# The second chunk of the first pass: from plain products to Strassen's seven, with its order around the first chunk's second stage and the sixth transposition

## The chip, the cores and the metric

One core of a Trainium2 chip. TensorE (PE in the profile, with its weight loads as PEld) does the matrix products, VectorE (DVE), ScalarE (ACT) and GpSimd (POOL) the elementwise work, and SyncE (SP) issues nearly all DMAs. The metric is device microseconds of one execution; the times of the kernel before are given as a median of four runs. Everything is fp32.

## The reference, cut to what matters

Causal attention with a decay and no softmax (8 batches, 8 heads, 576 tokens, 64 wide), whose output, 4608 tokens by 512, goes through a feed-forward block with a hidden width of 2048.

```python
scores = scale * np.matmul(q, k.transpose(0, 1, 3, 2))
Dmat = np.where(rel >= 0, gamma[:, None, None] ** rel[None, :, :], 0.0)
ret = np.matmul(scores * Dmat[None, :, :, :], v)
x = ret.transpose(0, 2, 1, 3).reshape(B * S, H * D)
h = x @ w_in
sp = np.maximum(h, 0.0) + np.log1p(np.exp(-np.abs(h)))
g = h * erf(sp)
return g @ w_out
```

## The kernel before, in words

**Attention.** The 4608 tokens are cut into 36 pieces of 128, numbered from 0. Each piece goes through three stages in a fixed list (`stages`): `transposes(i)` brings q and k into transposed form (qT, kT), `scores(i)` multiplies them on PE (L347, eight matmuls) and masks the product on DVE into sT (L352, recorded at L99), and `outputs(i)` makes the piece's output on PE (L365, L376, L388) and writes it, scaled, into the tile x on DVE. `attend` runs the list up to a given place. For pieces 0 to 7, q and k are transposed on PE (L332) and copied out by ACT; from piece 8 on, q is transposed on DVE in squares of 32 (L326), and from piece 12 on k too. `weigh_values(i)` multiplies v by a decay on POOL (L313): for pieces 0 to 7 inside `transposes(i)`, later inside `outputs(i - 1)`. Each call also issues the loads of a later piece on SP's queue. The sixth transposition is that of piece 5.

**Feed-forward.** Four pieces make a chunk of 512 tokens; there are nine chunks. The hidden width is done in four groups (g) of 512 columns, so there are 36 blocks (g, c); "the first pass" is g = 0, which runs while attention still makes x. Each block has a first stage (x times w_in, L496) and a second stage (times w_out, L604), between them ACT's Softplus and Erf (L565, L569) and DVE's product of the two (`multiply`).

**Strassen.** Both stages run as a 2 by 2 block product in seven block products (the Winograd form) in place of eight. One product is four 128x256 matmuls. It needs sums of blocks of x (`operands_x`: four DVE instructions for g = 0, each 128x512, the third of them in place) and sums of blocks of the weights (`sums_in`, `sums_out`: four each per group). `First.first`, `middle` and `last` issue the products in the order A11, A12; S2, S3, S1; S4, A22. Three results are added on DVE to what ACT copied out before (L514, L527, L535, recorded at L99). The other way, `First.plain` (L539), makes the eight products as 16 steps of two matmuls (L550) and needs no sums of x or of w_in. Before the change chunks 0 and 1 of the first pass are plain (`PLAIN = 2`), so what is stored of them for the later passes (`xd`) is x without sums, and a later pass makes all three sums of the four that are not stored.

**Weights.** w_in and w_out come as float64 words and are rounded to fp32 in a generator, `rounding`, one step at a time: two ACT instructions (L254, L255), then DVE steps at L259, L263, L267 and L272, then two products, on DVE for the first group's w_in and on POOL for the rest (L274, L275). Behind the last part of a weight stand its block sums as four more steps. `round_weights(n)` takes n steps. In the first group the sums of w_out (wb) come ahead of those of w_in (wa), both behind the last part of w_out.

**Order.** All engines run in the order in which the program issues: there is no scheduler. The order around the change is written by hand: the string at L754 (a: one attention stage; p: one plain step of chunk 0; digits: rounding steps; w: a load of weights; s: store of x; k: filling matmuls), and the loop at L774 to L784, which runs chunk 1's 16 plain steps with one attention stage at every second one and issues chunk 0's Softplus, Erf, `multiply` and `sums` in between. Then chunk 0's second stage starts (`seconds[0].first`), and the general loop at L789 takes over; it catches attention up by `attend(after_chunk(2))` ahead of chunk 2's sums, so that whatever the order was, all stages up to the outputs of piece 11 are out when chunk 2's first product begins.

Of the kernel before, what the change touches and what calls it, by code (L numbers as in the profile page):

```python
# [2 lines left out]

# [1 line left out]

# [49 lines left out]
def kernel(  # L55
# [16 lines left out]
    n_dc = D_MODEL // P  # L72
    OH = D_MODEL // 2
    FH = D_FF // 2
    GP = 2
# [22 lines left out]
    def tt(out, in0, in1, op):  # L98
        nc.vector.tensor_tensor(out=out, in0=in0, in1=in1, op=op)  # L99
# [50 lines left out]
    def load(i, names="qkv"):  # L150
        if i < len(pieces):
            t = loaded.setdefault(i, {})
            for name in names:
                src = {"q": q, "k": k, "v": v}[name]
                if name == "q" and i < SQUARES:
                    t["q"] = load_rows(i, "q", q, 2)
                elif name == "q":
                    t["qs"] = load_squares(i, "q", q)
                    if i >= SQUARES_K:
                        t["ks"] = load_squares(i, "k", k)  # L160
                elif name == "v" or i < SQUARES_K or len(pieces[i]) == 1:
                    t[name] = load_rows(i, name, src, 4)
# [29 lines left out]
    def parts():  # L192

        w2 = w_in.rearrange("(e c d) (h f) -> c e d h f", c=n_dc, d=D, h=2)
        for g in range(n_g):
            for dc in range(n_dc):
                a = A11 if dc < 2 else A12
                src = [(heads[(e + dc) % 2], w2[dc, e, :, :, 2 * g * GW : 2 * (g + 1) * GW]) for e in range(2)]

                yield src, "wa", g, a, dc % 2, ["wa"] if g > 0 and dc == n_dc - 1 else []  # L200
            for f in range(2):
                for j in range(GP):
                    ft = f * FH // P + g * GP + j
                    src = [(slice(0, P), w_out[ft * P : (ft + 1) * P, :].rearrange("p (h o) -> p h o", h=2))]
                    sums = (["wb"] if g > 0 else ["wb", "wa"]) if (f, j) == (1, GP - 1) else []
                    yield src, "wb", g, B21 if f else B11, j, sums

    def sums_in(a11, s3, a12, a22, s1, s2, s4):
# [9 lines left out]
    def sums_out(b11, t3, b21, b22, t1, t2, t4):  # L218
# [7 lines left out]
        yield  # L226

    coming = parts()
    words = []
    most_g = [1]  # L230

    def load_weights():
        part = next(coming, None)
        if part is not None:
            t = wraw.tile([P, 2 * WP], UINT32, tag="wraw", name="wraw")
            for rows, src in part[0]:
                nc.sync.dma_start(out=t[rows].rearrange("p (h f) -> p h f", h=2), in_=src)
            words.append((t, *part[1:]))
# [49 lines left out]
    def round_weights(n=1):  # L288
        for _ in range(n):
            next(round_step, None)  # L290
# [149 lines left out]
    done = [0]  # L440

    def before_chunk(c):

        return stages.index((outputs, c * PC)) if c < n_ch else len(stages)

    def after_chunk(c):

        return stages.index((outputs, (c + 1) * PC - 1)) + 1

    def attend(upto):  # L450
        while done[0] < min(upto, len(stages)):
            of, i = stages[done[0]]
            of(i)
            done[0] += 1

    PLAIN = 2

    def load_x(g, c):  # L460
        x[g, c] = x_tile()
# [2 lines left out]
    def store_x(c):  # L464
        nc.sync.dma_start(out=xd[c], in_=x[0, c][:, :n_dc])
# [3 lines left out]
    def operands_x(g, c):  # L469
        summed.add((g, c))  # L470
        t = x[g, c]
        b11, b12, b21, b22 = (t[:, 2 * d : 2 * d + 2, h * TH : (h + 1) * TH] for d in range(2) for h in range(2))
        t1, t2, t4 = (t[:, n_dc + j, :].rearrange("p (d i) -> p d i", d=2) for j in range(3))
        if g == 0 or c < PLAIN:
            tt(t1, b12, b11, ALU.subtract)
            tt(t2, b22, t1, ALU.subtract)
            tt(b12, b22, b12, ALU.subtract)
        else:
            tt(t2, b12, b11, ALU.add)
            tt(t1, b22, t2, ALU.subtract)  # L480
        if g == 0:
            store_x(c)
        tt(t4, b21, t2, ALU.subtract)
        x[g, c] = {A11: b11, A12: b21, S4: b22, A22: t4, S1: t1, S2: t2, S3: b12}
# [240 lines left out]
    firsts = [First(g, c) for g, c in order]  # L725
    seconds = [Second(f) for f in firsts]
# [8 lines left out]
    def keep_busy(n):  # L735
        for _ in range(n):
            nc.tensor.matmul(idle[:, :P], lhsT=ones, rhs=ones, start=True, stop=True)


    most = [before_chunk(2)]  # L740

    def run(steps, rounds=(), stages=1):

        for step, _ in enumerate(steps):
            attend(min(done[0] + stages, most[0]))
            round_weights(rounds[step] if step < len(rounds) else 0)
# [4 lines left out]

    for what in "alkakakawkakakawwaa3awa2aaa5ppappa5wwppa5ppawappwcppa5ppaaapp5s":  # L754
        if what == "a":
            attend(done[0] + 1)
        elif what == "p":
            next(products)
        elif what == "s":
            store_x(0)  # L760
        elif what == "l":
            load(2, "kv")
        elif what == "c":
            nc.sync.dma_start(out=cst[:, CONST_FIRST:], in_=consts[:, CONST_FIRST:])
        elif what == "w":
            load_weights()
        elif what == "k":
            keep_busy(2)
        else:
            round_weights(int(what))  # L770
    most[0] = before_chunk(3)
    attend(after_chunk(1))
    store_x(1)
    for step, _ in enumerate(firsts[1].plain()):  # L774
        if step % 2 == 0:
            attend(min(done[0] + 1, most[0]))
        round_weights(int(step > 1))
        if step == 1:
            firsts[0].softplus()
            firsts[0].erf()  # L780
        elif step == 5:
            firsts[0].multiply()
        elif step == 8:
            firsts[0].sums()  # L784
    seconds[0].begin()
    run(seconds[0].first(), (2, 2))
    firsts[1].softplus()
    most[0] = before_chunk(4)
    for b, nxt in zip(blocks[2:], blocks[3:] + [None]):  # L789
        n = order.index((b.g, b.c))  # L790
# [9 lines left out]
        elif n + 2 < n_s:  # L800
            f = firsts[n + 1]
# [62 lines left out]
```

## Time and profile before

| what | value |
|---|---|
| median of four runs | 1029.7 us (1028.82 to 1031.45) |
| the profiled execution, its own time | 1031.62 us |
| its span | 1029.8 us |
| PE matmul busy | 1019.5 us, 6348 records |
| PE weight load busy | 876.9 us |
| DVE busy | 668.3 us |
| ACT busy | 390.3 us |
| POOL busy | 123.6 us |
| granted TensorE clock, mean | 0.998 |

How to read it: each fp32 matmul of the program stands in the profile as two MATMUL records. 1.8 us of the profiled execution's time lie outside its span. A matmul record's duration overlaps the next one's, so for the cost of PE work the spacing from start to start is taken. The profile's line numbers are those of the kernel before.

### The profile page before, as it was taken

The numbers are of one execution on the slowest core, as the hardware profiler recorded it, in microseconds if no ns is written. First come the engines' busy times: TensorE is split into PE (matmuls) and PEld (weight loads), VectorE is DVE, ScalarE is ACT, GpSimd is POOL, SyncE is SP. The second block draws the span as 40 slices with busy tenths as digits, with TensorE's granted clock in tenths as the row PEclk, the third lists the DMA queues.
The fourth block names the chain that finished last, engine by engine and source line by source line (L and its number), as shares of the span: only waits on it lengthen the run. The fifth ranks groups of instructions, "written<-read, shape, count | busy, mean of one in ns | idle before, by whom it ended". The sixth has DMA issues, their size and how long they took to land.

```text
span 1029.8 us, 15959 instructions
## 1 busy us (share of the span) xinstructions
PE 1019.5 (99%) x6348; PEld 876.9 (85%) x6348; DVE 668.3 (65%) x1062; ACT 390.3 (38%) x481; POOL 123.6 (12%) x122
## 2 busy tenths in 40 slices
PE   9899999999999999999999999999999999999998
PEld 7687888888888888888888888888888888888887
DVE  3759878877876666666566666666657655555555
ACT  2254133232244544334343344444443333333332
POOL 2133121221311110000001001100100000000000
PEclk9999999999999999999999999999999999999999
DMA  9986979979984444444445344444433334444434
GB/s 197 203 235 147 247 155 246 230 172 244 233 191 151 165 144 143 144 155 166 159 147 170 143 143 144 156 168 147 143 123 123 123 124 131 131 132 131 128 85 120
DMA packets 146986, 165.76 MB, mean 161 GB/s; under 512 B 97376, under 2 KB 121568, under 8 KB 138848
## 3 DMA queue, kind: packets, MB, share of 16 engines
q1 hardware_dynamic: 144832, 163.57, 56.2%
q10 hardware_dynamic: 2080, 1.18, 0.5%
q8 instruction: 50, 0.82, 0.4%
q14 instruction: 24, 0.20, 0.1%
HBM read 117.52 MB, written 47.19 MB: 160 GB/s over the span
## 4 chain that ended last, share of the span: by engine, by line
PE 88%; DMA 4%; DVE 4%; SPq 2%; issue 1%; POOL 1%; ACT 0%; DVEq 0%; POOLq 0%; ACTq 0%
PE a L604 23%; PE a L496 22%; PE g L496 11%; PE g L604 11%; PE e L604 6%; PE e L496 5%; PE s L347 2%; PE o L365 2%; DMA wraw<-in_moe_w_in_dram 1%; PE o L388 1%; PE o L376 1%; SPq L147 1%; DMA raw_qs<-in_q_dram 1%; DMA raw_ks<-in_k_dram 1%; PE f L668 1%
## 5 line engine op out<-in xcount | busy, mean ns | idle before, releaser
L496 PE MATMUL a<-x,wa 128*128 128x256 f32 x1088 | 258.3, 380 | 0.0
L496 PEld LDWEIGHTS a<-x,wa 128*128 128x128 f32 x1088 | 205.7, 190 | 28.5
L604 PE MATMUL a<-wb,s 128*128 128x256 f32 x840 | 200.0, 381 | 0.0
L604 PEld LDWEIGHTS a<-wb,s 128*128 128x128 f32 x840 | 158.4, 190 | 23.0 <-ACT o L618 0.7
L99 DVE TENSOR_TENSOR t<-g,t 128x512 f32<-128x512 f32 x68 | 46.9, 690 | 150.4 <-ACT t L526 112.9
L496 PE MATMUL g<-x,wa 128*128 128x256 f32 x544 | 129.2, 380 | 0.0
L496 PEld LDWEIGHTS g<-x,wa 128*128 128x128 f32 x544 | 102.8, 190 | 14.4
L99 DVE TENSOR_TENSOR o<-a,o 128x512 f32<-128x512 f32 x104 | 71.5, 687 | 46.4 <-PE a L604 46.4
L521 ACT COPY t<-a 128x512 f32<-128x512 f32 x34 | 19.9, 586 | 188.3 <-PE a L496 188.3
L99 DVE TENSOR_TENSOR t<-t,s 128x1024 f32<-128x1024 f32 x72 | 88.9, 1275 | 0.0
L565 ACT ACTIVATE s<-t 128x1024 f32<-128x1024 f32 x72 | 72.1, 1049 | 28.5 <-DVE t L99 28.4
L274 POOL TENSOR_TENSOR wraw<-wraw 128x512 f32<-128x512 f32 x28 | 29.4, 1051 | 439.5 <-DVE wraw L272 177.9
L99 DVE TENSOR_TENSOR x<-x 128x512 f32<-128x512 f32 x115 | 75.8, 693 | 1.2
L532 ACT COPY t<-a 128x512 f32<-128x512 f32 x34 | 19.9, 586 | 144.3 <-PE a L496 144.3
L569 ACT ACTIVATE s<-s 128x1024 f32<-128x1024 f32 x72 | 72.1, 1048 | 0.4
L604 PE MATMUL g<-wb,s 128*128 128x256 f32 x280 | 66.7, 381 | 0.1
L604 PE MATMUL e<-wb,t 128*128 128x256 f32 x280 | 66.6, 380 | 0.0
L604 PE MATMUL a<-wb,t 128*128 128x256 f32 x280 | 66.6, 380 | 0.0
L604 PE MATMUL g<-wb,t 128*128 128x256 f32 x280 | 66.3, 380 | 0.0
L496 PE MATMUL e<-x,wa 128*128 128x256 f32 x272 | 64.8, 381 | 0.0
L99 DVE TENSOR_TENSOR sT<-s,cst 128x512 f32<-128x512 f32 x72 | 46.2, 682 | 28.5 <-PE s L347 28.5
L99 DVE TENSOR_TENSOR o<-g,o 128x512 f32<-128x512 f32 x70 | 47.9, 684 | 21.5 <-ACT o L618 18.8
(86 smaller groups left out, 1251.2 us busy)
## 6 DMA issues: line engine op xcount, KB each, us to landing
od<-o SPq DMA_DIRECT2D x54, 512.0 KB, 3.3
x<-xd SPq DMA_DIRECT2D x27, 1024.0 KB, 4.8
o<-od SPq DMA_DIRECT2D x27, 1024.0 KB, 5.4
raw_qs<-in_q_dram SPq DMA_DIRECT2D x96, 112.0 KB, 4.4
raw_ks<-in_k_dram SPq DMA_DIRECT2D x84, 112.0 KB, 4.1
xd<-x SPq DMA_DIRECT2D x9, 1024.0 KB, 5.2
raw_v<-in_v_dram SPq DMA_DIRECT2D x64, 128.0 KB, 4.5
wraw<-in_moe_w_in_dram SPq DMA_DIRECT2D x32, 256.0 KB, 6.0
```

Of the source, the lines that this page charges most:

```text
L99: nc.vector.tensor_tensor(out=out, in0=in0, in1=in1, op=op)
L147: queue.dma_start(out=t[r0 : r0 + n, e::2, :], in_=heads.rearrange("h p d -> p h d"))
L274: engine.tensor_tensor(out=r_f, in0=high_f, in1=r_f, op=ALU.mult)
L347: nc.tensor.matmul(ps[e][:, p, :], lhsT=t["kT"][heads[e], p, :], rhs=t["qT"][heads[e], p, :], start=True, stop=True)
L365: nc.tensor.matmul(o[p % 2][heads[(e + p) % 2], p // 2, :], lhsT=t["v"][:, 2 * p + e, :], rhs=t["sT"][:, e, p, :], start=(p < 2), stop=(no ...
L376: nc.tensor.matmul(o[p % 2][heads[(e + p) % 2], p // 2, r0 : r0 + m], lhsT=state[heads[e], p, :], rhs=t["qT"][heads[e], p, r0 : r0 + m], s ...
L496: nc.tensor.matmul(acc[:, j * TH : (j + 1) * TH], lhsT=weights["wa", self.g][:, a, d, j * P : (j + 1) * P], rhs=x[self.g, self.c][a][:, d, :],
L521: nc.scalar.copy(out=self.t1[:, 1], in_=self.a)
L532: nc.scalar.copy(out=self.t2[:, 0], in_=self.a)
L565: nc.scalar.activation(self.s[:, j], t, AF.Softplus)
L569: nc.scalar.activation(self.s[:, j], self.s[:, j], AF.Erf)
L604: nc.tensor.matmul(acc[:, tp, :], lhsT=left[:, j * TH + tp * P : j * TH + (tp + 1) * P], rhs=weights["wb", self.g][:, b, j, :], start=(sta ...
```

## The change

Chunk 1's first stage in the first pass goes by the seven products: its 16 plain steps become 7, with one attention stage ahead of each. `operands_x(0, 1)` is issued in front of them; it also stores the chunk, now with the in-place sum in it, so later passes make two sums of this chunk and not three. w_in's sums of the first group stand behind w_in's own last part, and the digit 4 in the string takes them. Chunk 0's Softplus and Erf, `multiply` and `sums` are issued at steps 0, 2 and 4. Softplus of chunk 1 is called by `last` and so comes ahead of chunk 0's second stage. In the string, the two plain steps that stood behind piece 5's transposition (`ppappa`) stand ahead of it (`ppppaa`).

```diff
-                yield src, "wa", g, a, dc % 2, ["wa"] if g > 0 and dc == n_dc - 1 else []
+                yield src, "wa", g, a, dc % 2, ["wa"] if dc == n_dc - 1 else []
...
-                    sums = (["wb"] if g > 0 else ["wb", "wa"]) if (f, j) == (1, GP - 1) else []
+                    sums = ["wb"] if (f, j) == (1, GP - 1) else []
...
-    PLAIN = 2
+    PLAIN = 1
...
-    for what in "alkakakawkakakawwaa3awa2aaa5ppappa5wwppa5ppawappwcppa5ppaaapp5s":
+    for what in "alkakakawkakakawwaa3awa2aaa5ppppaa5wwppa5ppawappwcpp4a5ppaaapp5s":
...
-    store_x(1)
-    for step, _ in enumerate(firsts[1].plain()):
-        if step % 2 == 0:
-            attend(min(done[0] + 1, most[0]))
-        round_weights(int(step > 1))
-        if step == 1:
+    operands_x(0, 1)
+    f = firsts[1]
+    for step, _ in enumerate(chain(f.first(), f.middle(), f.last())):
+        attend(min(done[0] + 1, most[0]))
+        round_weights((0, 2, 2, 2, 2, 3, 3)[step])
+        if step == 0:
             firsts[0].softplus()
             firsts[0].erf()
-        elif step == 5:
+        elif step == 2:
             firsts[0].multiply()
-        elif step == 8:
+        elif step == 4:
             firsts[0].sums()
     seconds[0].begin()
-    run(seconds[0].first(), (2, 2))
-    firsts[1].softplus()
+    run(seconds[0].first())
```

## The prediction

> **What bounds the kernel now.** I read the page's engine table and slices first.
>
> ```profile
> PE 1019.5 (99%) x6348; PEld 876.9 (85%) x6348; DVE 668.3 (65%) x1062; ACT 390.3 (38%) x481; POOL 123.6 (12%) x122
> PE   9899999999999999999999999999999999999998
> ```
>
> PE is the bound, and after the first slices it has no gap to give back: what this change is worth is PE work taken out, plus gaps closed, less gaps opened, between 29 and 104 us. The chain of waits gives the unit: eight records, four matmuls of 128x256, take 1.73 us, or 1.92 us behind an attention stage, so a matmul costs 0.432 us.
>
> Then PE's timeline around the sixth transposition, and, second, the windows of 3.41 us there, whose columns are length, busy time of the five engines with their instruction counts, granted clock, DMA share and GB/s.
>
> ```profile
> 29.70 1.99 PE L550 MATMUL p<-x,wa 128*128 128x256 f32 x8
> 34.34 0.63 PE L332 MATMUL pt_q<-ident,raw_q 128*128 128x128 f32 x4 [2.65 <-DMA raw_q<-in_q_dram]
> 35.56 0.88 PE L332 MATMUL pt_k<-ident,raw_k 128*128 128x128 f32 x4 [0.59 <-DVE wa L275]
> 36.24 1.91 PE L550 MATMUL pe<-x,wa 128*128 128x256 f32 x4
> 37.94 1.66 PE L550 MATMUL pg<-x,wa 128*128 128x256 f32 x4
> 39.53 1.09 PE L365 MATMUL o<-sT,raw_v 128*64 128x128 f32 x16
> ```
>
> ```profile
> 32.38:35.79 3.41, 0.85 (x6) 0.68 (x7) 2.92 (x5) 0.64 (x2) 0.00 (x0) 1.00 0.64 139
> 35.79:39.20 3.41, 3.41 (x11) 2.78 (x10) 0.00 (x0) 1.71 (x3) 1.04 (x1) 0.50 0.94 168
> ```
>
> PE waits 2.65 us for q and then for k (the page names DVE's wa, which the transposition doesn't read; the view of raw_k has its DMAs landing up to 7.1 us after issues at 27.7 and 28.4, about 35.4). A window in which PE was busy for 0.85 of 3.41 us is followed by one at half clock, where the two plain steps pe and pg take 3.16 us from start to start (the chain's 1.71 and 1.45) and not 1.73.
>
> Last, DVE's and POOL's timelines, for what the sums of x will meet.
>
> ```profile
> 66.46 0.41 DVE L99 TENSOR_TENSOR x<-o,cst 128x256 f32<-128x256 f32 x1
> 66.80 0.76 DVE L326 STREAM_TRANSPOSE qT<-raw_qs 128x256 f32<-128x256 f32 x2
> 81.04 1.78 DVE L99 TENSOR_TENSOR s<-t 128x512 f32<-128x512 f32 x1
> 104.52 3.53 DVE L99 TENSOR_TENSOR x<-x 128x512 f32<-128x512 f32 x4
> ```
>
> ```profile
> 66.02 1.04 POOL L274 TENSOR_TENSOR wraw<-wraw 128x512 f32<-128x512 f32 x1 [4.06 <-issue]
> 67.14 1.28 POOL L275 TENSOR_TENSOR wb<-wb,wraw 128x512 f32<-128x512 f32 x1
> 68.37 0.61 POOL L427 TENSOR_TENSOR state<-sums,cst 128x256 f32<-128x256 f32 x1
> 68.94 2.04 POOL L313 TENSOR_TENSOR raw_v<-raw_v,cst 128x512 f32<-128x512 f32 x2
> 80.84 1.42 POOL L275 TENSOR_TENSOR wb<-wb,wraw 128x512 f32<-128x512 f32 x1
> ```
>
> A DVE instruction with both inputs in SBUF takes 0.6 to 0.7 us alone. The one at 81.04 took 1.78: it ended 0.55 us after POOL's L275 (82.26). So while POOL works, such instructions alternate with POOL's.
>
> **The change, part by part.**
>
> *Sixth transposition.* pe and pg read x of pieces 2 and 3 (DVE done at 29.9) and w_in's first part, which the steps ahead of them read too, so they start at 31.43 and end at 33.16. q and k still land when they did: no DMA is issued earlier. The transposition ends at 35.56 + 0.44 = 36.0 at full clock, and the outputs of piece 4 start at 36.05 in place of 39.53: **-3.5 us**, of which 1.73 is cover and the rest the clock. The trace has a fall behind a window busy for 25% (0.85 of 3.41) and none behind one busy for 80% (2.74 of 3.42, the window before). With the windows where they lie here, PE is now busy for 0.85 + 0.78 us, 48%; lie they otherwise, the two idle stretches left (33.16 to 34.34, 34.83 to 35.56) fall into two windows, busy for 65% (1.18 idle) and more. If the clock falls all the same, it takes back half of 3.41 us, 1.7. I take full clock, as over these places the share is nearer to 80 than to 25; both ends stay. What is late next: DVE's rounding ahead of piece 5's mask, but that chain hangs on piece 4's outputs (DVE idle 5.17 us before 40.68) and moves with them; w_in's last part landed by 40.0 for a DVE step at 46.5.
>
> *w_in's sums.* Four DVE instructions (2.6 us; 3.81 in the trace, beside POOL) move from 94 to 99 into DVE's gap of 3.44 us at 51.1. Beside POOL's L427 and L313 they may delay piece 6's mask by 0.4 us, which its outputs, 1.5 us later on PE, don't see: 0.
>
> *Seven products for eight.* 28 matmuls for 32: 4 x 0.432 = **-1.73 us**. The three added DVE sums (0.69 each) read PSUM, and PE needs none of them.
>
> *Sums of x.* Four DVE instructions now stand between piece 7's x (66.88) and piece 8's qT, and piece 8's scores wait for qT on PE. Times are before's; all of it comes 3.5 us sooner. PE reaches those scores at 64.81 + 1.92 (A11) + 0.44 (k of piece 8) + 1.73 (A12) = 68.90. DVE alternates with POOL's five: sums end at 67.60, 69.29, 70.31 and 71.76 (each waits for the POOL instruction in hand, then takes 0.54; POOL's L275, L427 and L313 follow within 1.15, 0.5 and 0.9 us). qT takes 0.76: scores at 72.5, a wait of **+3.6 us**. Alone the four take 2.6 us, scores at 70.3, wait 1.4. At the rate of 104.52 (3.53 with POOL at work for the first 1.8) it is 2.3. I take 3.6: POOL's queue there is the trace's own, and full. The ACT copy of piece 8's k (67.8) isn't late.
>
> *The clock after that wait.* Between 0 and 1.7 us (half of 3.41). Moved 3.5 us up, the wait lies from 65.4 to 69.0; of the window from 66.51 to 69.92 PE would be busy for 0.9 us, 27%, next to the row with the fall, so I take one. It cost 3.16 - 1.73 = 1.43 us there on two plain steps alone: **+1.5**. [...]
>
> *Behind it.* The wait of 0.37 us at piece 10's scores (85.85, on DVE's qT) goes: qT comes 2 us ahead of its use, **-0.4**. The half microsecond at 91.9, where outputs of piece 10 wait for the mask, stays, as DVE's three remaining sums of wb now stand ahead of that mask. SP keeps its order; the store of chunk 1 waits for the third sum (70.3, not 66.9), and behind it the q loads of piece 10 wait for piece 8's qT as before, 5 us later (72.5 for 67.6); they landed 9 us ahead of their use at 85.0. POOL's order is unchanged. `attend` brings both orders together at piece 11. The three DVE sums saved in later passes meet no PE gap: 0.
>
> Sum: -3.5 - 1.7 + 3.6 + 1.5 - 0.4 = **-0.5**. The profiled execution, 1031.6, goes to 1031.1. It lies 1.9 over the median of the runs shown; I apply the difference to the median: **1029.2 us**. About 0.2% (2.06 us) is what a measurement of this kernel can tell from no change.
>
> **Rivals.**
> - *Faster: the wait is shorter, or the clock holds.* Clock full: -2.0, 1027.7; with a wait of 1.4 as well, -4.2, 1025.5. For it: the wait is one block that two windows may share. Against it: POOL's five instructions stand back to back from 66.02 to 70.98. 30%, most of it past 0.2%.
> - *Slower: DVE becomes the bound up to piece 10's outputs.* DVE is busy for 29.66 of 36.73 us from 66.88 to 103.61; it gains 2.1 of adds and up to 4.9 of sums and loses 3.8. The place is the rounding of w_out's last part: POOL's L275, then DVE's sums of wb, then the mask. Stepping DVE's new order on from 72.5 by the trace's durations (mask 1.3, `multiply` 2.35, four sums of s 2.6, qT 0.7, rounding steps 0.4 to 0.7), none ahead of the PE product or ACT copy that it reads, L272 of that part ends at 88.9, L274 and L275 at 91.8 (2.9 later, as from 86.7 to 89.6 in the trace), the sums at 94.5 and the mask at 95.7, against PE's need at 95.1. Each microsecond later is one on PE; 2.6 later, by five more instructions that alternate with POOL at 0.5 us each, gives -0.5 + 2.6 = +2.1, 1031.8 and more. Against it: DVE has 7 us of idle time there. 13%.
> - *The gain at the transposition is halved.* The window at 48% still brings a fall: -0.5 + 1.7 = +1.2, 1030.9. 12%.
> - Forecast, 1029.2, with 1028 to 1030.5 as its own range: 45%.
>
> **The numbers.** Faster by over 0.2% (under 1027.6): 27%, from the first rival. Slower by over 0.2% (over 1031.8): 12%, the second. Within: 61%. The range leaves out half of each outer case: 1026.0 to 1031.2.
>
> **What would show it.** Right: pe and pg start at about 31.5, no window at half clock from 35 to 39, piece 4's outputs at about 36; a PE gap of about 3.6 us ahead of piece 8's scores, named with DVE's qT, the four x sums just before it taking about 4.9 us, and a half-clock window behind it; chunk 2's first product about 2 us, or 0.5 with the fall, ahead of 103.61. Wrong: that gap under 1.5 us; a clock fall at 35; PE gaps named with wb or sT at 85 to 100; or any PE gap after 110 that the trace of before doesn't have.

## The result

The changed kernel takes **1032.47 us** (median of 35 runs, 1029.71 to 1034.31); the kernel before, beside it, 1030.89 (56 runs, 1028.55 to 1033.51). The ratio is **1.0014, 95% interval 1.0008 to 1.0019**: slower by about 1.5 us, inside the 0.2% that were called no change, and above the range of the forecast (1029.2; 1026.0 to 1031.2).

The page's engine table and PE's slices of the changed kernel:

```profile
PE 1017.8 (99%) x6340; PEld 878.0 (85%) x6340; DVE 672.6 (65%) x1066; ACT 390.0 (38%) x481; POOL 124.4 (12%) x122
PE   9989999999999999999999999999999999999998
```

Eight PE records fewer, that is four matmuls, and PE is still the bound; the hole has moved from the second slice (26 to 51 us) to the third (52 to 77 us). PE's timeline of the changed kernel around the sixth transposition (start, length, engine, line, operation, tiles; in brackets the idle time before it and what ended it):

```profile
31.81 1.03 PE L550 MATMUL pe<-x,wa 128*128 128x256 f32 x4
32.67 1.03 PE L550 MATMUL pg<-x,wa 128*128 128x256 f32 x4
34.81 0.63 PE L332 MATMUL pt_q<-ident,raw_q 128*128 128x128 f32 x4 [1.11 <-DMA raw_q<-in_q_dram]
35.86 0.63 PE L332 MATMUL pt_k<-ident,raw_k 128*128 128x128 f32 x4 [0.42 <-DMA raw_k<-in_k_dram]
36.42 1.09 PE L365 MATMUL o<-sT,raw_v 128*64 128x128 f32 x16
```

pe and pg lie in the wait and run at full clock (0.86 us from start to start). Piece 4's outputs start at 36.42, 3.11 us ahead of 39.53.

DVE's, POOL's and PE's timelines of the changed kernel at the sums of x:

```profile
64.00 4.85 DVE L100 TENSOR_TENSOR x<-x 128x512 f32<-128x512 f32 x4
68.78 0.76 DVE L326 STREAM_TRANSPOSE qT<-raw_qs 128x256 f32<-128x256 f32 x2
```

```profile
64.23 1.61 POOL L275 TENSOR_TENSOR wb<-wb,wraw 128x512 f32<-128x512 f32 x1
65.80 1.06 POOL L427 TENSOR_TENSOR state<-sums,cst 128x256 f32<-128x256 f32 x1
66.82 2.94 POOL L313 TENSOR_TENSOR raw_v<-raw_v,cst 128x512 f32<-128x512 f32 x2
```

```profile
64.10 1.89 PE L496 MATMUL e<-x,wa 128*128 128x256 f32 x8
69.68 1.55 PE L347 MATMUL s<-qT,kT 64*128 64x128 f32 x16 [3.69 <-DVE qT L326]
71.16 3.24 PE L496 MATMUL a<-x,wa 128*128 128x256 f32 x8
```

The four sums take 4.85 us beside POOL, qT stands behind them, and PE waits 3.69 us. The step after it takes 3.24 us, not 1.99. The windows of 3.41 us of the changed kernel (start and end, length, busy time of PE, PE's weight loads, DVE, ACT and POOL with counts, granted clock, DMA share, GB/s) show why, and that the fall at 35 us is gone:

```profile
32.38:35.79 3.41, 1.95 (x11) 1.23 (x9) 3.16 (x6) 0.81 (x2) 0.00 (x0) 1.00 0.56 118
35.79:39.20 3.41, 3.34 (x42) 3.01 (x43) 1.80 (x5) 2.05 (x4) 1.04 (x1) 1.00 0.77 164
...
66.89:70.30 3.41, 0.62 (x10) 0.65 (x12) 3.22 (x5) 3.38 (x4) 2.87 (x2) 1.00 1.07 369
70.30:73.72 3.42, 3.42 (x16) 2.75 (x14) 2.53 (x5) 2.40 (x4) 0.00 (x0) 0.50 1.19 343
```

Trace against trace, by the starts of three of PE's stages, the outputs of pieces 4, 7 and 12, and the end of PE's last instruction:

| stretch of PE | before | after | moved |
|---|---|---|---|
| up to piece 4's outputs (39.53; 36.42) | 39.53 | 36.42 | -3.11 |
| from there to piece 7's (62.51; 59.60) | 22.98 | 23.18 | +0.20 |
| from there to piece 12's (110.21; 110.61), where the seven products are | 47.70 | 51.01 | +3.31 |
| from there to the end of PE's last instruction (1026.23; 1027.15) | 916.02 | 916.54 | +0.52 |

So the traces tell the story the forecast told, -3.1 and then +3.3 where it had -3.5 and +3.0. With the small rows they come to +0.9; the medians differ by 1.5 us. The rest lies in what one trace can't show. Each execution has its granted clock recorded. One window of 3.41 us at half clock, called a fall below, takes 0.0017 off its mean (half of 3.41, of 1029.8), and the mean comes down a little further by the half clock behind PE's end (from 1029.07 us to the end of the span at 1029.8 in before's trace: 0.0004).

| granted clock | windows at half clock | before: executions, median | after: executions, median |
|---|---|---|---|
| 0.999 to 1.0 | none | 39 of 94, about 1029.0 | 1 of 47, 1031.4 |
| 0.998 | one | 55 of 94, 1030.59 | 21 of 47, 1030.79 |
| 0.996 to 0.997 | two | none | 25 of 47, 1032.58 |

(Before: four series beside the experiments. After: the first measurement and the two repeats below.) By these medians a fall costs 1.6 to 1.8 us (0.9 to 1.8 in the four series of before taken singly). Before has 0.59 falls per execution and after 1.51.

### The profile page after: what moved, and what is told of

Same layout as the page of the kernel before. It is cut to its first block, busy times and chain, and to the rows that moved or that the text cites. A ratio compares the mean times of both kernels' runs of the same rounds, so it can differ in the third digit from the quotient of the medians.

```text
span 1030.8 us, 15944 instructions
## 1 busy us (share of the span) xinstructions
PE 1017.8 (99%) x6340; PEld 878.0 (85%) x6340; DVE 672.6 (65%) x1066; ACT 390.0 (38%) x481; POOL 124.4 (12%) x122
## 4 chain that ended last, share of the span: by engine, by line
PE 92%; DMA 4%; DVE 1%; SPq 1%; issue 1%; POOL 0%; ACT 0%; DVEq 0%; POOLq 0%
PE a L604 23%; PE a L496 23%; PE g L496 12%; PE g L604 11%; PE e L604 6%; PE e L496 6%; PE s L347 3%; PE o L365 3%; PE o L388 1%; PE o L376 1%; DMA raw_v<-in_v_dram 1%; DMA raw_k<-in_k_dram 1%; DMA raw_ks<-in_k_dram 1%; PE f L668 1%; SPq L132 1%; SPq L148 1%
## 5 line engine op out<-in xcount | busy, mean ns | idle before, releaser
L496 PE MATMUL a<-x,wa 128*128 128x256 f32 x1120 | 267.6, 382 | 0.0
L496 PEld LDWEIGHTS a<-x,wa 128*128 128x128 f32 x1120 | 213.0, 191 | 29.3 <-issue 0.2
L496 PE MATMUL g<-x,wa 128*128 128x256 f32 x560 | 133.1, 381 | 0.0
L496 PEld LDWEIGHTS g<-x,wa 128*128 128x128 f32 x560 | 106.0, 190 | 14.4
L100 DVE TENSOR_TENSOR x<-x 128x512 f32<-128x512 f32 x116 | 78.8, 712 | 1.3
```

Source lines behind the costliest of these rows:

```text
L496: nc.tensor.matmul(acc[:, j * TH : (j + 1) * TH], lhsT=weights["wa", self.g][:, a, d, j * P : (j + 1) * P], rhs=x[self.g, self.c][a][:, d, :],
```

## Theory and rivals

**Theory.** Without the clock the change is worth nothing: what the transposition (1.7) and the four matmuls fewer (1.7) give is taken by the wait of 3.7 us ahead of piece 8's scores. That wait comes from DVE alternating with POOL in the sums of x (4.85 us for the four). The 1.5 us come from the clock: the wait brings 1.5 falls per execution, and the fall at the transposition that goes was there in only six executions of ten. **Rivals.** The transposition gives less than the trace says; the sums cost their time whatever POOL does; the loss sits later (waits at 238 and 277 us); or DVE is the bound from 60 to 92 us, so that any order loses.

## The experiments

Ratios are to the kernel before, run beside each.

**One part alone.** First kernel: the kernel before with only the string changed.

```diff
-    for what in "...aaa5ppappa5wwppa5...
+    for what in "...aaa5ppppaa5wwppa5...
```

> The kernel before with one part of the change: pe and pg, the last two plain steps of the first quarter, ahead of the sixth transposition (piece 5). Theory (all of the transposition's gain is real in every execution): piece 4's outputs come 3.1 us sooner, as in the changed kernel's trace, no window at half clock from 35 to 39 us, and the time falls by about 3.1 us against before. Rival (the clock's fall behind that wait is not in every execution of before): the cover of 1.7 us comes in all, the clock's 1.4 to 1.75 in a part of them, so about 2.0 to 2.6 us on the median. A second rival: waits further back (238 and 277 us) eat a part of it; then chunk 2's first product is 3 us sooner but the last product less.

Measured: 1027.50 us (11 runs), ratio 0.9980 (0.9971 to 0.9989), so -2.1 us. All 11 executions have a clock of 0.999 or 1.0. Its PE timeline:

```profile
32.08 1.03 PE L550 MATMUL pe<-x,wa 128*128 128x256 f32 x4
32.95 1.03 PE L550 MATMUL pg<-x,wa 128*128 128x256 f32 x4
33.81 0.60 PE L332 MATMUL pt_q<-ident,raw_q 128*128 128x128 f32 x4
34.62 0.63 PE L332 MATMUL pt_k<-ident,raw_k 128*128 128x128 f32 x4 [0.21 <-PE pt_q L332]
35.18 1.09 PE L365 MATMUL o<-sT,raw_v 128*64 128x128 f32 x16
```

q has landed when PE comes to it. The trace gains 4.4 us against 39.53, the median 2.1: the first rival's number. **The trace of before was one of the executions with the fall, and the forecast took it for all.** That trace also has a longer wait for q (2.65 us) than the second kernel below, which has the same order there (1.22 us).

**The other part alone.** Second kernel: the changed kernel with the string's first change undone.

```diff
-    for what in "...aaa5ppppaa5wwppa5...
+    for what in "...aaa5ppappa5wwppa5...
```

> The changed kernel with that part undone: pe and pg behind the sixth transposition again, the seven products and the four sums of x kept. Theory: +3.6 (wait ahead of piece 8's scores) + 1.5 (half clock behind it) - 1.7 (four matmuls fewer) - 0.4 (piece 10's scores) = +3.0 us against before, and with what the changed kernel's trace shows later (238 and 277 us: +0.6) up to +3.6. Rival (the transposition's gain is smaller than 3.1 in most executions): the sum of this and of the first kernel must still be +1.5, so +3.5 to +4 here. If it is under +2, the sums of x cost less than I said and the loss lies elsewhere.

Measured: 1034.19 us (5 runs), 1.0043 (1.0030 to 1.0056), +4.4 us. With -2.1 for the first kernel that makes +2.3, which with these intervals fits the +1.5. Four of five executions are at 0.996 or 0.997, two falls. In its trace both places have one:

```profile
31.63:35.04 3.41, 1.66 (x10) 1.03 (x9) 3.20 (x7) 0.85 (x2) 0.12 (x1) 1.00 0.82 152
35.04:38.45 3.41, 3.41 (x11) 2.86 (x10) 1.01 (x2) 1.70 (x3) 1.16 (x1) 0.50 0.81 166
69.17:72.59 3.42, 0.71 (x12) 0.74 (x14) 3.14 (x5) 3.39 (x4) 2.79 (x2) 1.00 1.20 335
72.59:76.00 3.41, 3.41 (x15) 2.65 (x12) 2.64 (x6) 2.29 (x4) 0.00 (x0) 0.50 0.86 258
```

From piece 7's outputs to piece 12's it takes 51.03 us (changed kernel 51.01, before 47.70). From there to the end it takes 916.00 us (before 916.02), so none of this kernel's loss lies later. Over all fourteen traces this last stretch lies between 915.2 and 917.1: at 915.2 to 916.0 in the three with chunk 1 plain, at 916.5 to 916.9 in the three of the changed kernel, at 915.2 to 917.1 in the other eight with the seven products. A few tenths of a microsecond there may be the change's; these traces can't tell.

**The idle wait filled.** Fourth kernel: matmuls on ones in PE's wait ahead of piece 8's scores, overwritten by the scores.

```diff
         ps = [ps_at.tile(...) for e in range(2)]
+        for _ in range(14 if i == 8 else 0):
+            nc.tensor.matmul(ps[0][:, 0, :], lhsT=ones, rhs=ones, start=True, stop=True)
```

> The changed kernel with 14 matmuls of 128x128 on ones (0.22 us each, 3.1 us) put into the wait ahead of piece 8's scores; they are overwritten by the scores. The wait for qT stays, only PE isn't idle in it. Theory (idleness brings the half clock, which costs 1.5 us): scores start when they did, the window behind is at full clock, 1.3 to 1.7 us less than the changed kernel. Rival (the half clock comes all the same, or it costs nothing as DVE is late anyway behind it): within 0.4 us of the changed kernel.

Measured: 1028.77 us (12 runs), 0.9990 (0.9980 to 1.0000), about 2.5 us less than the changed kernel by the ratios, and every execution at 0.999 or 1.0. All the changed kernel's falls, 1.51 per execution, thus hang on this one wait; at 1.6 us each they make 2.4 us. The expected 1.3 to 1.7 us counted one fall; the time alone, known to about 1 us, wouldn't decide between the two.

```profile
63.96 3.29 PE L346 MATMUL s<-ones 128*128 128x128 f32 x28
67.81 1.16 PE L349 MATMUL s<-qT,kT 64*128 64x128 f32 x16 [0.56 <-DVE qT L326]
68.90 1.99 PE L498 MATMUL a<-x,wa 128*128 128x256 f32 x8
```

The scores start 10.1 us after piece 7's outputs (57.73), as in the changed kernel (69.68 - 59.60), but the step behind them takes 1.99 us. The stretch to piece 12's outputs is 49.38 us, 1.63 less than the changed kernel's: one fall.

**The same in the kernel before.** Fifth kernel: fills at the sixth transposition.

```diff
                 pt = ps_at.tile([P, NP, P], FP32, tag="at", name=f"pt_{name}")
+                for _ in range({("q", 5): 11, ("k", 5): 2}.get((name, i), 0)):
+                    nc.tensor.matmul(pt[:, 0, :], lhsT=ones, rhs=ones, start=True, stop=True)
```

> The kernel before with 11 matmuls of 128x128 on ones (2.4 us) in the wait for q and 2 (0.4 us) in the wait for k of the sixth transposition; the transposition overwrites them. Nothing starts sooner, PE only isn't idle. Theory (what the change gains there is 1.7 us of cover and, in those executions of before that have it, a fall of the clock): all executions at a clock of 1.0, 1.0 to 1.7 us under before on the median, and about 1 us over the first kernel. Rival (the fall has nothing to do with the idle wait): the same clocks as before, no change.

Measured: 1028.84 us (11 runs), 0.9990 (0.9981 to 0.9999), -1.0 us, all executions at 1.0. That is 0.59 falls of 1.6 us. This kernel and the fourth, before and after without their falls, have the same ratio, 0.9990, each to about 0.1%: without the clock the change is worth nothing that these runs can tell. Piece 4's outputs start at 37.05, between 39.53 (before, with the fall) and 35.18 (first kernel, with the cover); start-up differs by up to 0.9 us between these traces, so the parts aren't read more finely.

**The sums out of qT's way.** Third kernel: A11 and A12 read x as it is; the sums stand behind piece 8's transposition.

```diff
-    operands_x(0, 1)
+    raw_x = x[0, 1]
+    x[0, 1] = {A11: raw_x[:, 0:2, :TH], A12: raw_x[:, 2:4, :TH]}
...
         attend(min(done[0] + 1, most[0]))
+        if step == 0:
+            x[0, 1] = raw_x
+            operands_x(0, 1)
```

> The changed kernel with piece 8's transposition of q ahead of the four sums of x on DVE: the first two of the seven products read parts of x as they are, so the sums are only wanted by the third. Theory (the sums ahead of qT are the whole loss): the gap of 3.7 us ahead of piece 8's scores and the half clock behind it go, 5.2 us less than the changed kernel, about 3.7 under before. Rival (DVE is the bound there whatever the order): the wait moves to the third product (second sum) or to piece 8's outputs (mask), 1 to 3 us of it, and the gain against the changed kernel is 2 to 3 us.

Measured: 1028.07 us (11 runs), 0.9982 (0.9973 to 0.9990), -1.9 us against before and 3.3 less than the changed kernel by the ratios. Wait and falls are gone (0.999 and 1.0 throughout), but the rival took a part, at a place that its expectation didn't name, the rounding of w_out's last part:

```profile
82.66 1.16 PE L347 MATMUL s<-qT,kT 64*128 64x128 f32 x16 [0.28 <-DVE qT L326]
83.75 1.13 PE L604 MATMUL e<-wb,t 128*128 128x256 f32 x4
86.47 1.13 PE L604 MATMUL e<-wb,t 128*128 128x256 f32 x4 [1.58 <-POOL wb L275]
```

The stretch of the seven products takes 48.35 us, still 0.65 more than before's 47.70, though PE has four matmuls less to do. It is the second rival of the prediction, at the place it named; in the changed kernel no such wait shows, as PE comes there 6.0 us later (the scores ahead of it at 88.66 us, not 82.66).

**POOL taken out of the sums' way.** Sixth kernel: the changed kernel, leaving out the low words of w_out's second part and the weighing of the values of pieces 8 and 9.

```diff
+        if i in (8, 9):
+            return
         if i < len(pieces) and i not in weighed:
...
+            if (name, g, slot, j) != ("wb", 0, B11, 1):
-            engine.tensor_tensor(out=r_f, in0=high_f, in1=r_f, op=ALU.mult)
-            engine.tensor_tensor(out=a_f, in0=a_f, in1=r_f, op=ALU.add)
+                engine.tensor_tensor(out=r_f, in0=high_f, in1=r_f, op=ALU.mult)
+                engine.tensor_tensor(out=a_f, in0=a_f, in1=r_f, op=ALU.add)
```

> The changed kernel with four of POOL's instructions left out that stand beside the four sums of x: the two of rounding w_out's second part (its low words are not added) and the weighing of the values of pieces 8 and 9; only one POOL instruction is left there. DVE's order is the changed kernel's. Theory (DVE alternates with POOL, which makes 4.9 us of 2.6): the sums take about 3 us, the wait ahead of piece 8's scores is 1.4 to 1.9 us and not 3.7, the clock falls in fewer executions; 2 to 4.5 us less than the changed kernel. Rival (the sums take their 4.9 us for another reason, so POOL's work is no part of the price): the wait stays over 3 us and the time within 0.5 us.

Measured: 1028.06 us (11 runs), 0.9980 (0.9971 to 0.9989), 3.4 us less than the changed kernel by the ratios. DVE and PE in it:

```profile
62.33 2.81 DVE L100 TENSOR_TENSOR x<-x 128x512 f32<-128x512 f32 x4
65.06 0.76 DVE L329 STREAM_TRANSPOSE qT<-raw_qs 128x256 f32<-128x256 f32 x2
```

```profile
65.97 1.16 PE L350 MATMUL s<-qT,kT 64*128 64x128 f32 x16 [1.66 <-DVE qT L329]
86.24 1.13 PE L607 MATMUL e<-wb,t 128*128 128x256 f32 x4 [0.70 <-POOL wb L276]
```

2.81 us for the sums in place of 4.85, 1.66 of wait in place of 3.69. The wait is 2.0 us shorter and the falls are gone (all executions at 0.999 or 1.0), but not all of that is gained. The stretch from piece 7's outputs to piece 12's takes 48.36 us, 2.65 less than the changed kernel's, where 2.03 of wait and 1.63 of fall went. One microsecond comes back, 0.70 of it in the second row, at the rounding of w_out's last part as in the third kernel. Beside 5.6 us of POOL's work (1.61 + 1.06 + 2.94 in the changed kernel) the four sums are thus 2.04 us dearer than with most of it left out.

**Rounding moved up.** Seventh kernel: the third one with other rounding steps.

```diff
-        round_weights((0, 2, 2, 2, 2, 3, 3)[step])
+        round_weights((1, 3, 2, 2, 3, 2, 3)[step])
```

> The third kernel (q of piece 8 ahead of the sums of x), and the steps of rounding that stand beside the seven products moved up by one to two steps (1, 3, 2, 2, 3, 2, 3 in place of 0, 2, 2, 2, 2, 3, 3), into the 1.2 us in which DVE sat idle at 69.5 us there. In the third kernel's trace the gain was given back by waits of 1.6 us for w_out's last part (POOL) and 0.3 to 0.4 at three places. Theory (the rounding is all that is late behind the sums): that wait goes, 1.5 us less than the third kernel, 3.5 us under before. Rival (DVE is the bound up to 92 us whatever the order): the wait moves to the sums of w_out or a mask and the time stays within 0.7 us of the third kernel.

Measured: 1031.45 us (11 runs), 1.0015 (1.0005 to 1.0025), 3.4 us worse than the third kernel. My theory of the rounding fell. POOL now works from 81.11 to 85.60, beside DVE's sums of s, and qT of piece 10 is behind them:

```profile
81.48 1.53 DVE L100 TENSOR_TENSOR s<-t 128x512 f32<-128x512 f32 x1
83.05 1.66 DVE L100 TENSOR_TENSOR s<-s,t 128x512 f32<-128x512 f32 x1
84.62 1.53 DVE L100 TENSOR_TENSOR s<-t,t 128x512 f32<-128x512 f32 x1
86.07 0.68 DVE L100 TENSOR_TENSOR s<-t,s 128x512 f32<-128x512 f32 x1
86.67 0.70 DVE L326 STREAM_TRANSPOSE qT<-raw_qs 128x512 f32<-128x512 f32 x1
```

```profile
87.52 2.08 PE L347 MATMUL s<-qT,kT 64*128 64x128 f32 x16 [3.35 <-DVE qT L326]
```

The first three sums take 1.5 to 1.7 us beside POOL, the fourth 0.68 alone. It is the changed kernel's fault once more, at another place, and with the clock in it too: ten of the eleven executions are at 0.996 to 0.998, and the trace has two windows at half clock from 86.41.

**The sums of s behind qT.** Eighth kernel: the seventh one with DVE's order changed further.

```diff
-        round_weights((1, 3, 2, 2, 3, 2, 3)[step])
+        round_weights((1, 3, 2, 2, 2, 0, 2)[step])
...
-        elif step == 4:
+        elif step == 5:
             firsts[0].sums()
...
-    run(seconds[0].first())
+    run(seconds[0].first(), (2,))
```

> The third kernel with DVE's order changed further back: the rounding steps of the seventh kernel (moved up), the four sums of s of chunk 1 behind piece 10's transposition of q and not ahead of it, and the last two sums of w_out behind piece 10's mask. In the seventh kernel's trace the sums of s beside POOL's rounding took 5.3 us with that transposition behind them, and PE waited 3.4 us for it. Theory (the same alternation of DVE with POOL is the price there too, and the order decides who waits): no PE wait over 0.6 us is left from 60 to 104 us, 1 to 2.5 us less than the third kernel, 3 to 4 us under before. Rival (DVE's work from 62 to 92 us doesn't fit beside PE in any order): a wait of 1 us or more comes back at a mask, or at w_out's sums, and the time is within 0.7 us of the third kernel, 1.5 to 2.5 us under before.

Measured: 1030.11 us (12 runs), 0.9994 (0.9983 to 1.0004): by the ratios 1.2 us over the third kernel, and no better than before. The wait moved again, now through ACT, whose Softplus waits for DVE's `t` behind the sums of s, and PE for ACT's copy behind the Softplus. ACT's and PE's timelines:

```profile
90.40 2.00 ACT L565 ACTIVATE s<-t 128x1024 f32<-128x1024 f32 x2 [7.43 <-DVE t L100]
92.31 0.56 ACT L618 COPY o<-a 128x512 f32<-128x512 f32 x1
```

```profile
92.93 3.65 PE L604 MATMUL a<-wb,s 128*128 128x256 f32 x8 [1.52 <-ACT o L618]
```

Three orders, and the trace of each has a wait of 1.5 us or more. That is the rival's side. It is weaker for this kernel: its trace is the longest of the twelve executions (1035.11 us), with a wait of 2.06 us for k at the sixth transposition besides, and so may not stand for them. That no order at all fits is not shown.

**The wait made longer.** Ninth kernel: the last sum of x made three times.

```diff
-        tt(t4, b21, t2, ALU.subtract)
+        for _ in range(3 if (g, c) == (0, 1) else 1):
+            tt(t4, b21, t2, ALU.subtract)
```

> The changed kernel with the last of the four sums of x made three times, same output: two more DVE instructions of 0.6 to 0.7 us ahead of piece 8's transposition of q; POOL is done by then. Theory (the wait is paid one for one on PE, and a wait that goes on into a window at half clock brings a second window): the wait goes from 3.7 to about 5.0 us, nearly every execution has a clock of 0.996 or 0.997 and the trace shows a fall of 6.83 us, not 3.41; 1.3 us for the wait and 0.5 to 0.8 more for the clock over the changed kernel. Rival (the fall's length doesn't hang on the wait): clocks as in the changed kernel, 1.3 us.

Measured: 1034.22 us (5 runs), 1.0038 (1.0025 to 1.0050), 2.5 us over the changed kernel by the ratios. The wait is 5.86 us, not 5.0, since POOL worked on to 68.35 and the first of the two (67.48) took 1.42. All executions are at 0.995 to 0.997, and the clock in the trace falls for three windows, one more than said:

```profile
63.31:66.72 3.41, 1.28 (x6) 0.77 (x5) 3.40 (x3) 3.38 (x4) 3.41 (x3) 1.00 1.17 360
66.72:70.13 3.41, 0.00 (x0) 0.00 (x0) 3.34 (x5) 3.38 (x5) 1.63 (x2) 0.50 1.19 298
70.13:73.55 3.42, 3.10 (x19) 2.73 (x20) 1.77 (x4) 1.15 (x3) 0.00 (x0) 0.50 0.93 298
73.55:76.96 3.41, 3.41 (x12) 2.77 (x11) 3.38 (x7) 0.59 (x1) 0.00 (x0) 0.50 0.30 86
```

**The changed kernel again.**

> The changed kernel once more, beside the others. The fill of the wait (fourth kernel) took the granted clock from 0.996 to 0.998 up to 1.0 in nearly all executions and more time than the 1.5 us I had for one fall. Theory: the wait ahead of piece 8's scores brings two falls of 3.41 us in over half of the executions, not one; then 1 us and more over before, clocks of 0.996 and 0.998 in the executions, and a trace at 0.996 shows two windows at half clock near piece 8. Rival: the second fall is at the transposition of piece 5 or elsewhere; then a trace at 0.996 shows it there.

Measured: 1030.78 us (11 runs), 1.0013 (1.0004 to 1.0023). Five executions are at 0.996 or 0.997, six at 0.998. The trace is one of the six and has one fall, at 69.53, behind the wait's end (68.29). It also shows the sixth transposition with q landing sooner than in the changed kernel's first trace (a wait of 0.20 us, not 1.11):

```profile
33.60 0.63 PE L332 MATMUL pt_q<-ident,raw_q 128*128 128x128 f32 x4 [0.20 <-DMA raw_q<-in_q_dram]
35.22 1.09 PE L365 MATMUL o<-sT,raw_v 128*64 128x128 f32 x16
```

> One more trace of the changed kernel. If this execution's clock is 0.996 or 0.997, the theory has two windows at half clock one after the other from about 68 us, the first beginning inside the wait ahead of piece 8's scores; the rival has the second one at the sixth transposition. At 0.998 it says nothing new.

Measured: 1031.52 us, 0.998, one fall at 68.95, wait's end at 68.31: nothing new, as said.

**The wait moved against the windows.** Tenth kernel: eight matmuls on ones ahead of piece 6's scores.

```diff
+        for _ in range(8 if i == 6 else 0):
+            nc.tensor.matmul(ps[0][:, 0, :], lhsT=ones, rhs=ones, start=True, stop=True)
```

> The changed kernel with 8 matmuls of 128x128 on ones (1.75 us, overwritten) ahead of piece 6's scores, so that all that follows is 1.75 us later and only that. In three traces of the changed kernel the fall of the clock began 0.6, 1.2 and 0.6 us after the end of the wait ahead of piece 8's scores and lasted one window of 3.41 us; in the kernel with two more sums it began inside the wait and lasted three. Theory (where the wait lies against windows of 3.41 us, counted from the clock's first rise, decides): the fall begins 0.3 to 1.2 us before the wait's end in the trace and lasts two windows, though the wait is as long as in the changed kernel; the granted clocks of the executions shift against the changed kernel's; the time is 1.75 us over the changed kernel's plus or minus 1 for the clock. Rival (only the wait's length decides): one window in the trace, clocks as in the changed kernel, 1.75 us over it, 3.1 over before.

Measured: 1033.19 us (11 runs), 1.0031 (1.0021 to 1.0041), 1.8 us over the changed kernel by the ratios. The wait is 3.69 us, as before, and ends at 70.19. The fall begins at 69.02, 1.17 ahead of that, and lasts two windows:

```profile
65.60:69.02 3.42, 0.90 (x5) 0.45 (x3) 3.42 (x3) 3.39 (x4) 3.42 (x4) 1.00 1.09 366
69.02:72.43 3.41, 2.24 (x17) 2.04 (x18) 1.76 (x5) 3.40 (x4) 1.25 (x1) 0.50 1.20 334
72.43:75.84 3.41, 3.41 (x9) 2.58 (x10) 3.38 (x7) 0.76 (x2) 0.00 (x0) 0.50 0.88 248
```

So a wait of one length brings one window or two, by where it meets them. The executions, four at 0.996 or 0.997 and seven at 0.998, are too few to tell a shift from the changed kernel's. An execution of the changed kernel itself with two windows was counted by its clock, and not seen in a trace.

## Why the forecast missed

- *Sixth transposition, -3.5:* the mechanism was right, the size was not. The trace gave -3.11, start-up being 0.3 later, and the fall at 35 us went; the two later traces of the changed kernel, with q there sooner, start piece 4's outputs at 35.22 and 35.24, 4.3 ahead of before's trace. The step that failed is the clock's part, 1.75, credited whole from one execution: only 55 of 94 have the fall, so it was worth 0.59 x 1.6 = 0.9. On the median the part alone is worth 2.1 (1.1 to 3.0 by the interval) where the sum had 3.5. That the clock held was in part luck: the forecast's own window of 48% lies on the falling side of the border found below. In the changed kernel's trace PE was busy for 55% of that trace's own window there (1.88 of 3.41 us, 32.76 to 36.17), and with q there sooner PE idles less.
- *Eight products to seven, -1.73; piece 10's scores, -0.4:* right as far as the sum of the stretch tells. From piece 7's outputs to piece 12's, 47.70 - 1.73 - 0.37 + 3.69 + 1.63 (the fall, by the fourth kernel) is 50.92; the trace has 51.01.
- *Sums of x, +3.6:* right, 3.69; sums of 4.85 us beside POOL, as worked out. The row at 81.04 carried it, and POOL was what made the price (sixth kernel).
- *The clock after that wait, +1.5, "so I take one":* **the step that failed most.** A window idle enough for a fall (27% forecast; 18, 36 and 18% in the three traces) and about the cost of one fall were right, but 25 of 47 executions have two. I placed the windows by one trace, where their phase changes from run to run (the clock's first rise lies 4.1 to 5.5 us after the start). The term should have been 1.51 x 1.6 = 2.4, or 0.9 more.
- *w_in's sums, 0; later passes, 0:* right as far as the traces tell; no place that waits is new. The waits for kT near 238 and 277 us are in before too (0.5 us in all) and vary between traces of one kernel (0.9 to 1.4 in three of the changed kernel).
- *The base:* the four runs gave 1029.7. Before's other series have 1029.32, 1029.79, 1030.31, 1030.42 and 1030.89. With 1030.89, the sum's own -0.5 gives 1030.4. About 1.2 us of the miss of 3.3 are this, and 2.0 the change. Of these the clock's two terms make 1.7: -1.75 + 1.5 = -0.25 in the forecast, (1.51 - 0.59) x 1.6 = +1.5 by the count.
- *Rivals:* the halved gain (12%, 1030.9) came nearest, by another reason: no fall at the transposition came back (none of the 23 executions of the first and fourth kernels has one), only fewer went than credited. DVE as the bound (13%) holds as soon as the first wait is gone (third kernel).

The best version is the first kernel: the quarter's two steps moved, the second chunk left plain. Its ratio is 0.9980 to before; by both ratios it is 0.34% under the changed kernel.

## What to carry

Where a term of a forecast is a fall of the clock, ask in how many executions it comes, from the granted clock of each run, before crediting or charging it whole. An instruction put ahead of a transposition on DVE is priced by what POOL does then (the four sums took 4.85 us beside POOL's work and 2.81 with most of it left out), and moving it helps as far as DVE has room where it goes: here it took back 3.3 us, and still none of three orders made the seven products a gain over the first kernel. When two parts go in together, run each alone: here one gained 2.1 us and the other lost it twice over.

## What the runs showed of the chip

In these traces the clock changes by windows of 3.41 us, counted from its first rise, the first record of full clock (5.07 us after the start in before's trace, 5.45 in the changed kernel's, 4.1 to 5.5 in all fourteen): before's fall begins 30.72 us behind it, nine windows, the changed kernel's 64.85, nineteen, and the second kernel's two falls (35.04 and 72.59) lie eleven apart. Up to 300 us the fourteen traces have a sharp border. All 11 windows at full clock in which PE was busy for 49% or less were followed by a fall (the second kernel's 1.66 of 3.41 is the uppermost). None at 51% or more was; the sixth kernel's is the lowest:

```profile
63.05:66.46 3.41, 1.75 (x14) 1.29 (x14) 3.31 (x7) 3.38 (x4) 0.00 (x0) 1.00 1.31 263
```

Back to full came only after a window busy throughout (3.41 of 3.41 in before, the changed kernel and the second kernel); 0.00 and 3.10 (ninth kernel), 2.24 (tenth) and 2.30 (seventh) of 3.41 each kept half clock for one more. An estimate from these rows: if the wait of 3.69 us may lie anywhere against the windows, a window is idle for more than half (1.71 us) when its end comes 1.7 to 5.4 us after the wait's start. If that end still lies in the wait, at 1.7 to 3.7, the next window isn't busy throughout either, and two are at half clock: 2.0 of 3.4 cases, 58%. Otherwise it is one. Counted were 53% and 45%. For before's transposition the waits differ too much between executions (q: 2.65 us in before's trace, 1.22 in the second kernel's) for such a reckoning; why 59% of the executions have the fall there stays open.
